# A long convolution and a state-space layer side by side: transposes moved to the DMA crossbar, wide VectorE operations, and the convolution's first stage spread out

## The chip, the cores and the metric

The kernel runs on one core of one Trainium2 chip. The metric is the device time of one execution in microseconds (us), median of several runs.

PE is the TensorE matmul engine (PEld its weight loads), DVE is VectorE, ACT ScalarE, POOL GpSimd and SP SyncE. SP and POOL mostly issue DMA here. SBUF and PSUM are the on-chip memories: the kernel keeps its operands in SBUF and its matmul results in PSUM. A crossbar transpose is a DMA instruction (`dma_start_transpose`) that transposes a matrix while it loads it. The granted clock is the share of its full clock that the profile shows for PE.

## The reference

Two independent layers over 2048 positions and 1024 channels, in bf16, written side by side into one output:

```python
# A: short shift convolution (4 taps), gate, 2048-long convolution by FFT, gate
k_shift = sum(k_pad[:, t:t + S] * shift_k[:, 3 - t] for t in range(4))
kv = k_shift * v
y  = irfft(rfft(kv, 2 * S) * rfft(ssm_k, 2 * S))[:S] + kv * ssm_D
a  = q * y
# B: complex diagonal state space, 1024 states
Bu = x @ B_bar.T                      # B_bar, Lam_bar from Lambda, B, dt
h[t] = Lam_bar * h[t - 1] + Bu[t]
b  = 2 * (h @ C.T).real + x * Dskip
out = concatenate([a, b], axis=-1)
```

## The kernel before

**Layer B** goes in 16 chunks of 128 positions. For each chunk: `pu = B x` on PE (128 matmuls of 128 columns), a rotation by the angles of the states on DVE, two real scans on DVE (`tensor_tensor_scan`, 2.28 us each), a rotation back, and `py = C h` on PE (512 columns wide). x, B and C must stand transposed in SBUF; PE does it:

```python
def b_xT(i, eng="s"):
    pt = ps_t.tile([P, ND, P], BF16, name="pt")
    for dd in range(ND):
        nc.tensor.transpose(pt[:, dd, :], xn[:, dd * P:(dd + 1) * P], ident[:])
    ...                                   # copied to xT by ACT
# bt_prep and ct_prep: the same for B (16 blocks) and C (16 blocks)
```

A rotation is six DVE operations (four multiplies, two adds), each 1024 wide, one half of it being

```python
nc.vector.tensor_mul(ta, u[:, 0], ci); nc.vector.tensor_mul(tb, u[:, 1], si)
nc.vector.tensor_add(ta, ta, tb)
...                                       # tb: the imaginary part, the same way
```

**Layer A** goes in three stages. A1: the taps (four multiplies, three adds and the gate, 1024 wide, on DVE), matmuls with DFT matrices, results `Ys_kv` and `Ys_h` stored to DRAM. A2: 32 groups; load `l2k`, `l2h`, matmul, product on DVE (two 1024-wide multiplies), matmul, store `Vs`. A3: 16 rows; load `vv` and `q`, matmul, multiply, store. Each stage reads back what the one ahead of it stored, so they run one after the other.

**The schedule** is a fixed list of ticks, 8 for each chunk of B. Instructions are emitted tick by tick and each engine runs its own in that order:

```python
A1_STEP, A1H_STEP, A2_STEP, A3_STEP = 2, 2, 2, 1      # ticks per row or group
# A1 rows at ticks 0, 2, 4 ...; A2 after A1; A3 after A2
for n2 in range(N2):                      # A1
    b = A1_T0 + int(n2 * A1_STEP)
    ...                                   # loads at b - 4, taps at b, matmuls at b + 2
A2_T0 = a1_last + 6
for g in range(NG):
    b = A2_T0 + g * A2_STEP
    ...
A3_T0 = a2_last + 8
```

So A1 takes ticks 0 to 33, A2 39 to 106, A3 114 to 131, and B ends at 136: the three stages of A are spread over the whole of B.

## Time and profile before

| | |
|---|---|
| time | 432.85 us (profiled execution: span 431.1) |
| first rotation starts / last gate multiply of A1 starts (DVE) | 37 / 171 us |
| first A2 matmul with `l2k` / last store of `Vs` issued | 193 / 363 us |
| last rotation starts a multiply with `ci` | 392 us |

Stretches of the kernel before: busy time of PE, PEld, DVE, ACT and POOL (with the number of instructions), granted TensorE clock, DMA share and GB/s, at the start and at the end:

```profile
0.00:20.00 20.00, 7.91 (x89) 7.04 (x90) 11.42 (x44) 10.27 (x12) 5.32 (x13) 0.99 0.84 264
20.00:40.00 20.00, 16.57 (x231) 15.28 (x231) 17.84 (x55) 15.59 (x32) 0.00 (x0) 0.83 0.82 270
40.00:60.00 20.00, 17.02 (x255) 14.95 (x253) 20.00 (x35) 18.62 (x28) 5.14 (x9) 1.00 0.96 329
60.00:80.00 20.00, 19.37 (x228) 15.09 (x226) 20.00 (x36) 20.00 (x33) 9.81 (x15) 1.00 0.84 274
...
400.00:420.00 20.00, 15.85 (x67) 6.38 (x66) 11.47 (x17) 9.48 (x18) 4.88 (x9) 0.91 0.94 361
420.00:440.00 20.00, 5.08 (x26) 2.18 (x24) 0.69 (x1) 1.31 (x3) 1.08 (x2) 0.91 0.10 39
```

PE's "busy" includes pipelined matmuls waiting on one another, so it hides slack. A sharper figure is the count of matmuls times the spacing at which they follow each other when nothing holds them up: 0.0558 us for 128 columns, 0.109 for 256, 0.2158 for 512, the means of the uninterrupted pairs in this trace. By that count the kernel has **357 us of matmul work in a span of 431**, so PE is idle for 74 us.

### The profile page before, as it was taken

How to read it: one execution, taken by the hardware profiler on the slowest of the kernel's cores; microseconds unless marked ns; L12 is line 12 of the kernel's file. 1: busy time of each engine (PE TensorE's matmuls, PEld its weight loads, DVE VectorE, ACT ScalarE, POOL GpSimd, SP SyncE). 2: the span in 40 equal slices, each digit the busy share in tenths (PEclk: the TensorE clock that was granted, in tenths of full speed). 3: DMA queues.
4: the chain of work that ended last, by engine and by line, in shares of the span. 5: the costliest groups of instructions: out<-in, count | busy, mean ns of one | idle time of the engine just before them, and what ended most of it. 6: DMA issues, size and time to landing. Idle time of an engine off the chain costs nothing.

```text
span 431.1 us, 9757 instructions
## 1 busy us (share of the span) xinstructions
PE 380.7 (88%) x3713; PEld 259.7 (60%) x3713; DVE 350.7 (81%) x642; ACT 303.6 (70%) x531; POOL 130.2 (30%) x224
## 2 busy tenths in 40 slices
PE   2589799797987997999899999999899999997784
PEld 2578687575765875775556566566465666763331
DVE  2989999999999999936897979797959637976830
ACT  1977999787886887646678877878568783344451
POOL 4000344464654455311222232322122211012121
PEclk9979999999999899999999999999899999999989
DMA  7879987778776544397778687879666523959981
GB/s 247 285 255 309 336 289 254 265 240 249 276 235 205 167 163 159 120 334 238 229 241 263 217 247 245 265 234 295 195 217 181 165 69 135 298 176 396 403 316 73
DMA packets 41353, 102.23 MB, mean 237 GB/s; under 512 B 6621, under 2 KB 8925, under 8 KB 41306
## 3 DMA queue, kind: packets, MB, share of 16 engines
q1 hardware_dynamic: 27322, 58.60, 42.7%
q0 software_dynamic: 13984, 43.01, 28.8%
q8 instruction: 29, 0.48, 0.5%
q14 instruction: 18, 0.15, 0.1%
HBM read 59.64 MB, written 33.55 MB: 216 GB/s over the span
## 4 chain that ended last, share of the span: by engine, by line
PE 42%; DVE 28%; issue 12%; DMA 10%; ACT 5%; POOL 2%; SPq 0%; POOLq 0%; DVEq 0%; ACTq 0%
PE pu L274 13%; PE py L345 13%; DVE m L409 5%; PE psa L508 5%; DVE acc L410 4%; DMA hb<-ha 3%; PE psa L533 3%; PE psa L532 3%; DVE ta L305 2%; DVE tb L308 2%; DVE acc L414 2%; DMA out_dram<-ot 2%; POOL out_dram L88 2%; DMA bn<-in_B_C_re_dram 1%; PE pt L601 1%
## 5 line engine op out<-in xcount | busy, mean ns | idle before, releaser
L274 PE MATMUL pu<-xT,BT 128*128 128x128 bf16 x2048 | 156.1, 222 | 0.5 <-ACT xT L263 0.3
L274 PEld LDWEIGHTS <-BT 128*128 128x128 bf16 x2048 | 136.2, 100 | 33.5 <-issue 2.4
L345 PE MATMUL py<-CT,h 128*128 128x512 bf16 x512 | 140.2, 382 | 2.3 <-ACT yo L355 2.3
L345 PEld LDWEIGHTS <-h 128*128 128x128 bf16 x512 | 46.7, 98 | 45.5 <-issue 4.9
L88 POOL DMA_DIRECT2D hb<-ha x64 | 33.4, 526 | 88.9 <-ACT ha L509 85.0
L534 ACT CAST vsb<-psa 128x512 bf16<-128x512 f32 x64 | 37.0, 602 | 25.7 <-PE psa L533 24.8
L88 POOL DMA_DIRECT2D Ys_h<-ysbh x64 | 45.6, 716 | 30.8 <-ACT ysbh L475 29.4
L277 ACT CAST u<-pu 128x512 bf16<-128x512 f32 x64 | 39.4, 615 | 13.2 <-PE pu L274 13.1
L428 ACT CAST ysb<-psa 128x512 bf16<-128x512 f32 x64 | 38.5, 644 | 13.7 <-PE psa L427 13.3
L519 DVE TENSOR_TENSOR ha<-x,ha 128x1024 bf16<-128x1024 bf16 x32 | 21.9, 684 | 27.8 <-DMA hb<-ha 18.7
L475 ACT CAST ysbh<-psa 128x512 bf16<-128x512 f32 x64 | 38.7, 641 | 5.5 <-issue 2.3
L509 ACT CAST ha<-psa 128x512 bf16<-128x512 f32 x64 | 36.8, 598 | 7.3 <-PE psa L508 6.3
L509 ACT CAST x<-psa 128x512 bf16<-128x512 f32 x64 | 36.9, 593 | 7.3 <-PE psa L508 5.2
L308 DVE TENSOR_TENSOR_SCAN tb<-rtab,tb 128x1024 bf16<-128x1024 f32 x16 | 36.6, 2285 | 0.0
L305 DVE TENSOR_TENSOR_SCAN ta<-rtab,ta 128x1024 bf16<-128x1024 f32 x16 | 36.5, 2280 | 0.0
L427 PE MATMUL psa<-acc,F1t 128*128 128x512 bf16 x64 | 24.6, 392 | 12.0 <-DVE acc L414 11.9
L564 ACT CAST ot<-psa 128x512 bf16<-128x512 f32 x32 | 17.9, 589 | 24.4 <-DMA out_dram<-ot 14.8
L409 DVE TENSOR_TENSOR m<-krow,wbc 128x1024 bf16<-128x1024 bf16 x48 | 32.4, 675 | 0.0
L410 DVE TENSOR_TENSOR acc<-acc,m 128x1024 bf16<-128x1024 bf16 x48 | 32.3, 673 | 0.0
L532 PE MATMUL psa<-ha,wts 128*128 128x512 bf16 x64 | 24.5, 384 | 4.2 <-DVE ha L519 4.0
L88 POOL DMA_DIRECT2D Ys_kv<-ysb x32 | 17.8, 557 | 33.9 <-ACT ysb L428 33.9
L350 PE MATMUL py<-Dd,xT 128*128 128x128 bf16 x128 | 28.0, 219 | 0.0
(139 smaller groups left out, 628.5 us busy)
## 6 DMA issues: line engine op xcount, KB each, us to landing
Ys_kv<-ysb POOLq DMA_DIRECT2D x32, 256.0 KB, 2.9
Ys_h<-ysbh POOLq DMA_DIRECT2D x64, 128.0 KB, 3.3
l2k<-Ys_kv SPq DMA_DIRECT2D x16, 512.0 KB, 6.0
l2h<-Ys_h SPq DMA_DIRECT2D x16, 512.0 KB, 4.2
hb<-ha POOLq DMA_DIRECT2D x64, 128.0 KB, 3.7
Vs<-vsb POOLq DMA_DIRECT2D x16, 512.0 KB, 5.9
vv<-Vs SPq DMA_DIRECT2D x32, 256.0 KB, 6.6
xn<-in_B_x_dram SPq DMA_DIRECT2D x16, 256.0 KB, 4.3
```

Source lines behind the costliest of these rows:

```text
L88: return nc.gpsimd.dma_start(out_, in_)
L274: nc.tensor.matmul(pu[:, c, jl, :], BT[:, j, c, dd, :], xT[:, dd, :], start=(dd == 0), stop=(dd == ND - 1))
L277: nc.scalar.copy(u[:, :, j - 1:j + 1, :], pu[:])
L305: ops.append(lambda: nc.vector.tensor_tensor_scan(fl(st["ta"]), fl(rtab), fl(st["ta"]), 0.0, ALU.mult, ALU.add))
L308: nc.vector.tensor_tensor_scan(fl(st["tb"]), fl(rtab), fl(st["tb"]), 0.0, ALU.mult, ALU.add)
L345: nc.tensor.matmul(py[:], h[:, c, j, :], CT[:, j, c, dh * 512:(dh + 1) * 512], start=(j == 0 and c == 0), stop=(j == NJ - 1 and c == 1))
L409: ops.append(lambda jj=jj: nc.vector.tensor_mul(st["m"][:], krows[n2 - jj][:], wbc[:, jj, :]))
L410: ops.append(lambda: nc.vector.tensor_add(st["acc"][:], st["acc"][:], st["m"][:]))
L428: nc.scalar.copy(ysb[:, dh * 512:(dh + 1) * 512], pt[:])
L475: nc.scalar.copy(ysbh[:, :, n2l, :], pt[:].rearrange("p (c d) -> p c d", c=2))
L509: nc.scalar.copy(d_[:, dh * 512:(dh + 1) * 512], pt[:])
L532: nc.tensor.matmul(pt[:], wts[:, gi, 1, :], ha[:, dh * 512:(dh + 1) * 512], start=True, stop=False)
```

## The change

The intent: take the transposes off PE and the copies behind them off ACT; make VectorE's operations fewer and wider; and, since A1 was limited by VectorE while PE waited, spread A1 over twice as many ticks so that both engines are used evenly.

```diff
-    def b_xT(i, eng="s"):            # PE transpose, copy by ACT
+    def b_load_x(i):
+        nc.sync.dma_start_transpose(xT[:], x[i * T:(i + 1) * T, :])
+    def bt_load(j, c):
+        nc.sync.dma_start_transpose(BT[:, j, c, :, :], Bv[c][:, j, :])
+    def ct_load(c, hf):
+        nc.sync.dma_start_transpose(CT[:, :, c, hf * 512:(hf + 1) * 512], Cv[c][hf * 512:(hf + 1) * 512, :])
+    U_PRO = cfg.get("u_pro", 3)      # was 1: chunks of pu in the prologue
...
+    def win(Z):                      # overlapping windows of one table: [Z0 Z1], [Z1 Z2]
+        z = Z[:].rearrange("p a j t -> p (a j t)")
+        return bass.AP(z.tensor, z.offset, [list(z.ap[0]), [W, 2], [1, 2 * W]])
+        def rot_mul(src, Z):         # one 4096-wide multiply in place of four
+            s_ = src[:].rearrange("p b j t -> p (b j t)").unsqueeze(1).to_broadcast([P, 2, 2 * W])
+            nc.vector.tensor_mul(m, s_, win(Z))
...                                   # then one 2048-wide add; the scans stay
+            nc.vector.tensor_mul(st["m"][:, 0:h0, :], kring[:, s0:s0 + h0, :], wbc[:, 0:h0, :])
...                                   # taps: k rows in a ring of 8, one multiply (two at the wrap)
+        nc.vector.tensor_mul(hab[:], x16[:].unsqueeze(1).to_broadcast([P, 2, D]), hab[:])
...
-    A1_STEP = cfg.get("a1_step", 2.0)
+    A1_STEP = cfg.get("a1_step", 4.0)
-    A1H_STEP = cfg.get("a1h_step", 2)
-    A2_STEP = cfg.get("a2_step", 2)
+    A1H_STEP = cfg.get("a1h_step", 4)
+    A2_STEP = cfg.get("a2_step", 1.75)
```

With these steps A1 takes ticks 0 to 63, A2 69 to 128, and A3 begins at tick 136, when B has ended. The number of `u` buffers falls from 5 to 4; PSUM moves one buffer from the transposes to A (3 to 4).

## The prediction

> **What bounds the kernel now.** The stretch table shows five stages. 0–37 us, prologue: weights loaded and transposed on PE. 37–180, stage A1: DVE is busy 141.6 of 143 us and is the limit; PE's matmuls wait for DVE's `acc`. 180–200: PE fills up with `pu`. 200–358, stage A2: PE busy 153 of 158 (DVE 126, ACT 121). 358–431, tail: B's last four chunks until about 405, and A3, which ends as a stream of loads and stores (DMA share 0.94 in 400–420).
>
> **What the change does.**
> - PE: 384 transposes go (xT, BT, CT). In the chain of waits 16 back-to-back 128-column matmuls take 0.89 us, so about 21 us of real PE time. Their copies leave ACT (42 us of records) and DVE (6 us). SP issues crossbar transposes instead, 12 MB in all.
> - DVE: a 1024-wide bf16 multiply takes 0.68 us of record, about 0.63 net of overlap. At 2 elements a cycle ("VectorE: DVE Perf Modes", side-by-side) I estimate 2.2 us for 4096 and 1.2 for 2048. The widened operands are rows re-read at step 0, which "Vector Engine (DVE) Microarchitecture Reference" section 5.1 says keep the double rate; this trace has no such bf16 case. A chunk's rotation falls from about 12.9 to 11.6 us (both 2.28 us scans stay), a tap step from 5.1 to 4.7, A2's product from 1.27 to 1.2: about 27 us less DVE in all, of 351.
> - Schedule: A1 lasts 8 chunks instead of 4.25 and overlaps more B. A3 now starts after B, alone.
>
> **Critical path (estimates).** Prologue, three chunks of `pu`: first rotation at 38 us. A1: 8 × (11.6 + 2 × 4.7) = 168 us, DVE-bound; PE has about 150 us there. Switch: 9. A2: 88 us PE-bound while `pu` runs (2.5 us a tick), then 52 us at DVE's 2.15 us a tick; it ends near 353. Tail: last store of Vs 6 us, first load 6, 16 MB at about 380 GB/s 42: 52 us. Total 405. The gain is mostly balance: PE idles less behind DVE in A1, and 21 us of PE and 27 us of DVE work are gone; about 20 us is given back because A3 no longer overlaps B.
>
> **Prediction: 405 us, 80% range 384 to 430. Faster by over 2%: 0.80; within 2%: 0.13; slower by over 2%: 0.07.**
>
> **What would show each step right or wrong.**
> - 4096-wide multiplies at 2.2–2.3 us, not 4.3.
> - DVE busy near 320 us, at least 95% of A1, which lasts 165–175 us.
> - About 3330 PE matmuls; A2 with PE above 90% at first, then DVE.
> - In the tail PE nearly idle, DMA above 0.85, 45–60 us from the last `vsb` store to the end.
> - Crossbar transposes of 256 KB landing 1 to 1.5 us apart. "DMA: Bandwidth & Descriptors" gives 261 GB/s effective; this trace shows none.
>
> **What would make it wrong.** The transposes are the largest risk: at 100 GB/s the prologue's 4.75 MB and CT's 4 MB behind it on the same queue would hold back the first `pu`, the parameters (their transpose now stands behind the first `pu` matmuls) and the fourth chunk's x (behind CT), on which PE's fixed order waits before A1's matmuls: 440 or more. If wide operands lose the double rate, the kernel is far slower. If A2, where PE, ACT and DVE are within about 10% of each other, couples badly through four PSUM buffers, add 10–15 us. A shorter tail or quicker prologue gives 385.

## More of the kernel before

The kernel before takes 432.85 us in the runs taken with the kernel after. In the later sessions, on five chips, it took 430.3 to 434.4 us. Each experiment is therefore compared with the kernel before **of its own session**.

The page of the kernel before: the engines (busy time, share of the span, instructions), then the span in 40 slices of 10.8 us (each digit is the busy share in tenths):

```profile
PE 380.7 (88%) x3713; PEld 259.7 (60%) x3713; DVE 350.7 (81%) x642; ACT 303.6 (70%) x531; POOL 130.2 (30%) x224
...
PE   2589799797987997999899999999899999997784
...
DVE  2989999999999999936897979797959637976830
ACT  1977999787886887646678877878568783344451
...
DMA  7879987778776544397778687879666523959981
```

DVE is full from slice 2 to 17 (the prologue's end and A1), and PE from then on. PE's row stays at 7 to 9 up to slice 39. That is because B's last chunks lie on top of A3.

Two groups of instructions of the kernel before, by line (busy us, mean ns of one):

```profile
L519 DVE TENSOR_TENSOR ha<-x,ha 128x1024 bf16<-128x1024 bf16 x32 | 21.9, 684 | 27.8 <-DMA hb<-ha 18.7
...
L409 DVE TENSOR_TENSOR m<-krow,wbc 128x1024 bf16<-128x1024 bf16 x48 | 32.4, 675 | 0.0
```

## The result, and the profile after

The kernel after takes **452.38 us** against 432.85: 4.8% **slower**. The result is correct. Ratios, here and below, are the mean time of one kernel's fast runs over that of the other's of the same rounds, so not quite the ratio of the medians; here it is 1.0479 (95% interval 1.043 to 1.053).

The page of the kernel after, the same rows as before (40 slices of 11.2 us):

```profile
PE 374.3 (83%) x3329; PEld 242.8 (54%) x3329; DVE 329.8 (73%) x339; ACT 269.0 (60%) x496; POOL 133.5 (30%) x231
...
PE   0567919899899899979999699899999879985773
...
DVE  0374399999999999999999494997878888302221
ACT  1098306567477575838564478868889677823342
...
DMA  7999999967554856444367959868889894569993
```

The removed work is gone: 384 matmul records fewer, ACT 35 us and DVE 21 us less. But PE's row begins later and has a hole at slice 6, and DVE's row is low until slice 5 and again in the last six.

Groups of the kernel after, by line, answering to the two of before:

```profile
L524 DVE TENSOR_TENSOR hab<-x,hab 128x2048 bf16<-128x2048 bf16 x32 | 39.0, 1222 | 32.1 <-DMA hab<-hab 25.1
...
L303 DVE TENSOR_TENSOR mt<-u,Z 128x4096 bf16<-128x4096 bf16 x16 | 36.6, 2286 | 5.1 <-ACT u L288 5.0
...
L407 DVE TENSOR_TENSOR mt<-kring,wbc 128x4096 bf16<-128x4096 bf16 (+3 forms) x16 | 30.3, 1892 | 0.9 <-DMA kring<-in_A_k_dram 0.3
```

The wide operations run as predicted: 2.29 us for 4096 elements and 1.22 for 2048, against 0.68 for 1024.

Stretches of the kernel after, start and end:

```profile
0.00:20.00 20.00, 3.36 (x29) 2.96 (x30) 1.17 (x10) 1.49 (x2) 9.00 (x20) 1.00 0.91 176
20.00:40.00 20.00, 16.29 (x209) 15.62 (x207) 12.39 (x56) 15.52 (x25) 0.00 (x0) 0.83 1.10 191
40.00:60.00 20.00, 13.23 (x178) 12.68 (x176) 11.00 (x18) 9.35 (x20) 0.49 (x1) 0.83 1.18 229
60.00:80.00 20.00, 14.10 (x179) 13.24 (x179) 19.47 (x16) 8.15 (x15) 4.03 (x6) 0.74 1.06 253
...
400.00:420.00 20.00, 12.79 (x35) 3.37 (x33) 4.15 (x6) 7.41 (x14) 3.80 (x7) 0.66 1.01 378
420.00:440.00 20.00, 14.11 (x32) 3.23 (x32) 5.54 (x8) 8.21 (x16) 4.08 (x8) 0.57 1.05 400
```

In the first 80 us the DMA engines show a busy share of 0.91 to 1.18 (the profile's figure can pass 1) and move 176 to 253 GB/s, less than before (264 to 329). After 400 us they move 378 to 400 GB/s with 32 to 35 matmuls in 20 us: that is A3 nearly alone (B's last matmul with C starts at 401 us), at a DMA share of 1.01 to 1.05.

The waits of PE in the first 80 us of the kernel after (us in total, times, longest). The 13.7 us are the wait for the very first x; the first `pu` matmul of the kernel before started at 12.2 us, so little of that one is new:

```profile
PE pu L285 <- DMA xT<-in_B_x_dram: 21.8, 2, 13.7
PE pu L285 <- DMA BT<-in_B_B_im_dram: 4.6, 2, 2.9
```

**Where the 18.5 us of span went.** By the count of matmul spacings, the kernel after has 336 us of matmul work in 449.6, so 114 us idle against 74:

| | before | after | difference |
|---|---|---|---|
| matmul work | 357 | 336 | −21 |
| PE idle, first 80 us | 29 | 46 | +17 |
| PE idle, 80 to 400 us | 32 | 33 | +2 |
| PE idle, after 400 us | 13 | 35 | +21 |
| span | 431 | 450 | +19 |

(The differences are of the unrounded values.) Idle here is all time beyond the count at full spacing, so a slower PE counts as idle too. The granted clock was lower after the change: 0.74 to 0.83 from 20 to 80 us (before: 0.83, then 1.00), and 0.66 and 0.57 after 400 us (before: 0.91). An estimate from the start times of the matmul records in the two traces: matmuls that followed one another at up to 2.25 times their spacing took 11 us beyond it in the first 80 us against 5 before, and 7 against 2 after 400 us. So some 5 us of each loss may be a slow clock. Whether the clock follows the waits or adds to the loss, no run tests.

The change saved what it promised on PE. By this count it lost it at the start, and as much again at the end. A count of idle time does not show which of it moves the end; the experiments ask that.

### The profile page after: what moved, and what is told of

The parts are those of the page before. It is cut to its first block, busy times and chain, and to the rows that moved or that the text cites. A ratio compares the mean times of both kernels' runs of the same rounds, so it can differ in the third digit from the quotient of the medians.

```text
span 449.6 us, 8585 instructions
## 1 busy us (share of the span) xinstructions
PE 374.3 (83%) x3329; PEld 242.8 (54%) x3329; DVE 329.8 (73%) x339; ACT 269.0 (60%) x496; POOL 133.5 (30%) x231
## 5 line engine op out<-in xcount | busy, mean ns | idle before, releaser
L285 PE MATMUL pu<-xT,BT 128*128 128x128 bf16 x2048 | 146.5, 229 | 28.4 <-DMA xT<-in_B_x_dram 21.8
L321 DVE TENSOR_TENSOR_SCAN g<-rtab,g 128x1024 bf16<-128x1024 f32 x32 | 72.6, 2282 | 0.3
L524 DVE TENSOR_TENSOR hab<-x,hab 128x2048 bf16<-128x2048 bf16 x32 | 39.0, 1222 | 32.1 <-DMA hab<-hab 25.1
L88 POOL DMA_DIRECT2D hab<-hab x64 | 33.3, 525 | 88.8 <-ACT hab L517 74.5
L537 ACT CAST vsb<-psa 128x512 bf16<-128x512 f32 x64 | 36.5, 611 | 21.8 <-PE psa L536 18.2
L483 ACT CAST ysbh<-psa 128x512 bf16<-128x512 f32 x64 | 37.2, 626 | 14.8 <-PE psa L482 11.3
L571 DVE TENSOR_TENSOR ot<-ot,qt 128x1024 bf16<-128x1024 bf16 x16 | 11.1, 692 | 41.4 <-ACT ot L567 41.4
L517 ACT CAST hab<-psa 128x512 bf16<-128x512 f32 x64 | 36.5, 606 | 6.9 <-PE psa L516 5.8
L303 DVE TENSOR_TENSOR mt<-u,Z 128x4096 bf16<-128x4096 bf16 x16 | 36.6, 2286 | 5.1 <-ACT u L288 5.0
L303 DVE TENSOR_TENSOR mt<-g,Z 128x4096 bf16<-128x4096 bf16 x16 | 36.5, 2281 | 0.0
L535 PE MATMUL psa<-hab,wts 128*128 128x512 bf16 x64 | 25.1, 393 | 11.5 <-DVE hab L524 11.4
L407 DVE TENSOR_TENSOR mt<-kring,wbc 128x4096 bf16<-128x4096 bf16 (+3 forms) x16 | 30.3, 1892 | 0.9 <-DMA kring<-in_A_k_dram 0.3
```

The source lines that it names most:

```text
L88: return nc.gpsimd.dma_start(out_, in_)
L285: nc.tensor.matmul(pu[:, c, jl, :], BT[:, j, c, dd, :], xT[:, dd, :], start=(dd == 0), stop=(dd == ND - 1))
L303: nc.vector.tensor_mul(m, s_, win(Z))
L321: nc.vector.tensor_tensor_scan(g[:, a * W:(a + 1) * W], rt1, g[:, a * W:(a + 1) * W], 0.0, ALU.mult, ALU.add)
L407: nc.vector.tensor_mul(st["m"][:, 0:h0, :], kring[:, s0:s0 + h0, :], wbc[:, 0:h0, :])
L483: nc.scalar.copy(ysbh[:, :, n2l, :], pt[:].rearrange("p (c d) -> p c d", c=2))
```

## The experiments

Two theories stood at first. **S**: the schedule is the loss; spreading A1 pushes A2 and A3 back until A3 runs alone. **X**: the crossbar transposes are the loss; they deliver late and slow down the loads beside them. Fifteen kernels were run. Chips differ by up to 1%, so the ratio to the same session's kernel before is given with each time.

### 1. The change with the old steps

```diff
-A1_STEP 4.0, A1H_STEP 4, A2_STEP 1.75
+A1_STEP 2.0, A1H_STEP 2, A2_STEP 2
```

> The changed kernel with only the schedule of stage A1 and A2 put back (a tap step and an h step every 2 ticks, a product step every 2 ticks), so that A3 again overlaps the last chunks of B. Theory S (the spread leaves A3 alone at the end with PE idle): A1 shrinks from 171 us to about 125, A2 starts near 200 and ends near 350, the end comes about 60 us after A2's end; 410 to 420 us, 7 to 9% faster than the changed kernel (452). Theory X (the crossbar transposes are what costs): within 2% of the changed kernel, about 450. First rotation stays near 53 us under both.

Measured: **454.9 us, ratio 1.0524** (1.045 to 1.060), correct. Theory S's 410 to 420 us failed outright. Undoing the schedule alone gives nothing. A1 now takes 141 us (52.9 to 193.6) against 134 in the kernel before (37 to 171), though its VectorE operations cost less. The waits of this kernel between 60 and 140 us show the stall:

```profile
DVE hT L469 <- ACT hT L465: 11.5, 2, 7.3
...
PE pu L285 <- DMA xT<-in_B_x_dram: 7.6, 1, 7.6
...
DVE mt L407 <- DMA kring<-in_A_k_dram: 3.6, 1, 3.6
```

PE stood still for a late x (58 to 66 us). DVE's waits for `hT` come at 95 to 102 us and before 137 us; that the late x sets them off through PE's fixed order is not shown by this trace. Experiment 6, the same steps with ordinary loads, shows that they belong to the crossbar: there the wait for the fourth x falls to under 1 us, the wait for `hT` falls from 11.5 to 3.4 us, and A1 takes 12 us less.

### 2. The change with ordinary loads instead of crossbar transposes (wrong result)

```diff
-nc.sync.dma_start_transpose(xT[:], x[i * T:(i + 1) * T, :])
+nc.sync.dma_start(xT[:], x[i * T:(i + 1) * T, :].rearrange("p (a b) -> p a b", a=ND))
 # B and C the same way; same bytes, same tiles, not transposed
```

> Wrong result on purpose: the changed kernel with every crossbar transpose (x, B, C) replaced by an ordinary load of the same bytes into the same tile; all else is unchanged. Theory X: the first rotation moves from 52.7 us to about 38 to 40, DMA share in the first 80 us falls well below 1, PE no longer waits for x, and the whole kernel gains 12 to 20 us (432 to 440). Theory S: at most 5 us gained, because the end is set elsewhere. If the gain is 12 to 20 us and not more, the transposes explain only a part.

Measured: **441.03 us, ratio 1.0218** (1.015 to 1.029). The result is wrong as intended. The first rotation starts at 45.8 us instead of 52.7, and in the first 40 us the loads move 269 and 366 GB/s instead of 176 and 191. The 7 us at the first rotation reach the end of A1 (216 us instead of 224), and A2 ends 10 us earlier (384 instead of 394). So the crossbar costs 11 us against transposes that cost nothing at all; both time and first rotation lie a little outside the ranges of theory X (432 to 440, and 38 to 40). That is a bound and no alternative: a correct kernel has to transpose somehow. And 9 us of loss remain.

### 3. The kernel before with the new steps alone

```diff
-A1_STEP 2.0, A1H_STEP 2, A2_STEP 2
+A1_STEP 4.0, A1H_STEP 4, A2_STEP 1.75      # b = A2_T0 + int(g * A2_STEP)
```

> The kernel before with only A1 spread over 64 ticks and A2 at 1.75 ticks (nothing else of the change). Theory S: A1 lasts 8 x (12.9 + 2 x 5.1) = 185 us, ends near 222, A2 starts near 244 and ends near 395, A3 alone 55 us: 445 to 460 us, 3 to 6% slower than before. Theory X: the schedule alone is neutral or better, 425 to 435.

Measured: **447.45 us, ratio 1.0344** (1.028 to 1.041), correct. The schedule alone costs the kernel before 15 us. Theory S is right in this direction.

### 4. The kernel before with the wide VectorE operations alone

The rotations, taps and A2's product of the change, with PE transposes and the old steps. To make room, `u` has 4 buffers, the ring of k rows 6, and the rows of x, B and C share one pool.

> The kernel before with only the wide DVE operations (rotations over the Hankel tables, 4096-wide taps, 2048-wide product); transposes stay on PE, A1 stays at 34 ticks. To fit in memory it has 4 buffers for u, freed early, a tap ring of 6 rows, and x, B and C rows share 4 buffers. Theories S and X both expect the DVE-bound A1 stage to shrink by about 12 us (141 to 129) and the tail's rotations by about 5: 413 to 422 us, 3 to 4% faster. The rival that the wide operations are themselves what costs (they hold the engine for 2.3 us and delay the short ones that others wait for): 430 or more.

Measured: **427.35 us, ratio 0.9896** (0.984 to 0.996), correct. A1's last gate multiply starts at 163 us instead of 171, 8 us earlier, but the first A2 matmul with `l2k` only 1.5 us earlier (191.2 against 192.7), and the whole gains 5 (4.5 by the ratio). That lies between the two expectations, 413 to 422 and 430 or more. In between PE's record is full (39.6 of 40 us busy in 160 to 200; 37.2 before), which suggests that PE limits there and that most of VectorE's gain only lets VectorE wait.

### 5. The change with a faster A2

```diff
-A2_STEP 1.75
+A2_STEP 1.25
```

> The changed kernel with one number altered: a product step of A2 every 1.25 ticks instead of 1.75, so that A2 ends about 2 chunks of B earlier and A3 has B's last chunks beside it again. Theory S (the tail where only A3 is left costs about 20 us of idle PE): A2 takes about 125 us instead of 148, ends near 370, the tail is 60 to 68 us: 430 to 440 us. Rival (A2 is held by its own chain of product, swap DMA and copies, so it cannot run faster, whatever the step says): A2's end stays near 390 and the time near 450.

Measured: **436.58 us, ratio 1.0143** (1.008 to 1.021), correct: about 15 us gained by one number (3.4 points of ratio). Last stores of `Vs`, after the change and here (line, count, duration, first and last start):

```profile
L88 POOL DMA_DIRECT2D Vs<-vsb x16: 538/572/574, 265.2 to 394.2; - x16
```

```profile
L88 POOL DMA_DIRECT2D Vs<-vsb x16: 537/572/574, 266.9 to 381.9; - x16
```

A2 ends 12 us earlier, and A3 now lies over B's last chunks: its loads start at 385 us and B's last matmul with C at 421 us (after the change: 397 and 401). The time from the last store of `Vs` to the end is the same, 56 us against 55. So B's last chunks fit beside A3 at no cost. The cost of leaving A3 alone at the end is thereby shown, not only argued.

### 6. Ordinary loads and the old steps together (wrong result)

The edits of 1 and 2 in one kernel.

> Wrong result on purpose: ordinary loads in place of the crossbar transposes together with the A1 and A2 steps of the kernel before. The crossbar version of this schedule took 455 us, 17 us above what I expected of A1 (141 against 125) and 22 above in A2. If the slow crossbar loads in the first 70 us are the reason that the dense A1 fails: A1 back to 125 to 130 us, 415 to 425 in all. If the smaller buffers (one PSUM buffer for transposes, four for u) or DVE's fixed order are the reason: A1 still 135 us or more, 440 or more.

Measured: **433.59 us, ratio 1.0071** (1.001 to 1.013). A1 takes 129 us (46.1 to 174.8), as the first expectation said, but the time missed its 415 to 425. Under the old steps the crossbar costs about 20 us (4.5 points of ratio), not 11: the parts of the change do not add. And transposes that cost nothing still leave this kernel 1.75 points, some 7 us, behind the one of experiment 4, which transposes on PE. That remainder is not the crossbar's; the two differ in the prologue (three chunks against one), its order, the PSUM buffers and the ring of k rows, and no run separates these.

### 7. The change with a one-chunk prologue

```diff
-U_PRO = cfg.get("u_pro", 3)
+U_PRO = cfg.get("u_pro", 1)
```

> The changed kernel with one chunk of u in the prologue instead of three; the crossbar loads are the same. If the first rotation waits for the landing of the last B tile (about 40 us): it stays at 43 to 46 us, 7 to 9 earlier than 52.7, and A1 ends that much earlier; the rest is unchanged, so 443 to 448. If the two chunks that are no longer prepared leave PE behind in A1 (DVE waits for u): no gain or a loss, 450 to 460.

Measured: **465.48 us, ratio 1.0809** (1.077 to 1.085), correct. The first rotation starts at 42.5 us, ten earlier, and the kernel is still about 14 us slower. PE has 33 matmul records in 40 to 60 us against 178: the three-chunk prologue is what PE has to do while transposes land. A1 ends 5 us later (228 us against 224), since DVE waits inside it, for u (4.9 us) and for k rows (6.4 us). So an earlier first rotation is worth something where the next chunks' u is ready, as in experiment 2, and nothing where it is not, as here.

### 8. Crossbar for C and for x after the first chunk, PE for the rest

Built on 4 (wide operations, old steps).

> The wide DVE operations with the schedule of the kernel before; B and the first x tile still transposed on PE, C and the other x tiles by crossbar. It takes 248 of the 384 transposes (about 14 us of PE) and about 34 us of ACT copies out of a kernel that PE limits after its first 200 us, and keeps the prologue's path free of crossbar loads. If the change's parts are sound and only their prologue and schedule are not: 410 to 418 us (before_wide 427). If crossbar loads cost as much as they save wherever they stand (a DMA queue held for 4 to 8 us by each C tile, late x): 425 or more.

Measured: **431.75 us, ratio 1.0012** (0.997 to 1.006), correct: about 5 us slower than 4 (1.16 points of ratio), though 14 us of PE and some 30 us of ACT work were taken away. Stretches of this kernel (the profiled run was its slowest, 436.5 us):

```profile
40.00:60.00 20.00, 13.88 (x182) 11.84 (x180) 19.83 (x17) 9.99 (x19) 5.08 (x8) 0.91 1.18 236
60.00:80.00 20.00, 14.92 (x121) 10.19 (x121) 11.04 (x12) 10.40 (x20) 7.33 (x11) 0.83 1.07 303
```

The DMA engines are full while C is transposed, and DVE has work for only 11 of 20 us in the second stretch (it waited 6.8 us for k rows). In this arrangement the crossbar gains nothing net. That it loses at the loads beside it what it saves on the engines is read from these stretches and not tested.

### 9. The transposes by themselves (a measuring kernel, wrong result)

```python
for i in range(16): nc.sync.dma_start_transpose(xt[i][:], xv[i])       # 256 KB each
for i in range(15, -1, -1): nc.sync.dma_start(xt[i]..., xv[i])         # the same bytes, plain
for i in range(15, -1, -1): nc.sync.dma_start_transpose(xt[i][:], xv[i])
# sixteen ordinary loads of k, 256 KB each, on the POOL queue
```

> A measuring kernel, wrong result on purpose, no comparison of times wanted: sixteen 256 KB crossbar transposes of x with nothing beside them, then the same 4 MB by ordinary loads on the same queue, then the transposes again with ordinary loads of k on the other queue. Theory X (the crossbar itself has a low rate, whatever runs beside it): the first phase takes 26 to 32 us, 130 to 160 GB/s, as the first 37 us of the changed kernel did, the ordinary loads 12 to 16 us, and the third phase is hardly longer than the first. Rival (the crossbar is as fast as ordinary loads by itself, and lost its rate in the changed kernel to the loads beside it): the first phase takes under 18 us, and only the third falls to 140 GB/s.

The loads of k were meant to stand beside the third phase, but 14 of the 16 were issued in the first 18 us, so the phases changed places: the **first** has loads beside it, the **third** nearly none. Landings are read from the small VectorE copy that waits for each tile (start, duration):

```profile
0.74 39.58 SPq L95 DMA_TRANSPOSE xt<-in_B_x_dram  x16
...
5.00 0.15 DVE L91 CAST z<-xt 128x1 f32<-128x1 bf16 x1 [5.00 <-DMA xt<-in_B_x_dram]
...
25.99 0.15 DVE L91 CAST z<-xt 128x1 f32<-128x1 bf16 x1 [3.52 <-DMA xt<-in_B_x_dram]
...
49.79 0.15 DVE L91 CAST z<-xt 128x1 f32<-128x1 bf16 x1 [0.50 <-DMA xt<-in_B_x_dram]
50.46 0.15 DVE L91 CAST z<-xt 128x1 f32<-128x1 bf16 x1 [0.51 <-DMA xt<-in_B_x_dram]
...
63.03 0.15 DVE L91 CAST z<-xt 128x1 f32<-128x1 bf16 x1 [0.80 <-DMA xt<-in_B_x_dram]
...
78.12 0.15 DVE L91 CAST z<-xt 128x1 f32<-128x1 bf16 x1 [0.91 <-DMA xt<-in_B_x_dram]
```

- Beside loads: the first 4 transposes took 26 us, while 3.7 MB of k went through. Together that is 4.7 MB at about 182 GB/s: the loads, too, went far below their own rate.
- After the loads, in the same phase: the other twelve landed from 25.99 to 42.72, 1.39 us apart. So the slow stretch went with the loads and not with the place of the phase.
- Nearly alone: from 63.03 to 78.12 eleven more landed, 1.37 us each, **191 GB/s**.
- Ordinary loads: from 49.79 to 55.87 nine landed, 0.68 us each, **388 GB/s**.

Both theories of the rate were half right. In this one run the crossbar by itself has half the rate of ordinary loads, and beside ordinary loads it falls far behind. The kernel after fits both (issues on SP's queue: start, duration):

```profile
2.20 1.34 SPq L139 DMA_TRANSPOSE BT<-in_B_B_re_dram  x1
3.58 3.31 SPq L133 DMA_TRANSPOSE xT<-in_B_x_dram  x1
6.93 4.35 SPq L139 DMA_TRANSPOSE BT<-in_B_B_im_dram  x1
11.31 5.47 SPq L133 DMA_TRANSPOSE xT<-in_B_x_dram  x2
16.84 1.31 SPq L139 DMA_TRANSPOSE BT<-in_B_B_re_dram  x1
18.19 1.31 SPq L139 DMA_TRANSPOSE BT<-in_B_B_im_dram  x1
...
38.83 8.03 SPq L142 DMA_TRANSPOSE CT<-in_B_C_re_dram  x1
```

Up to 16.8 us SP got five transposes out, beside the first loads on the other queue. From then on it issued one every 1.35 us (one took an us longer), the pace of the measuring kernel. The 19 transposes of x and B, 5.0 MB, thus took 35 us.

### 10. The change with the fourth and fifth x ahead of C

```diff
-                at(tu - 12, "misc", lambda i=i: b_load_x(i))
+                if i >= U_PRO + 2:
+                    at(tu - 12, "misc", lambda i=i: b_load_x(i))
...
+    for i in (U_PRO, U_PRO + 1):
+        b_load_x(i)
     for hf in range(2):
         for c in range(2):
             ct_load(c, hf)
```

> The changed kernel with the x of the fourth and fifth chunk transposed ahead of the four 1 MB transposes of C instead of behind them. The tensor engine waited 8.0 us for the fourth chunk's x at 58 to 66 us. If that wait is on the way to the end, 446 to 450 us instead of 452; if the time before the first rotation and the loss of overlap at the end are all that counts, it stays within 2 us of 452.

Measured: **452.2 us, ratio 1.0478** (1.042 to 1.054), correct: nothing. PE's wait for that x is gone (its 21.8 us for x in the first 80 us fall to 16.4, all of it the first x), and by the count PE does 5 us more work there; A1 still ends at 223 us. So these 5 us of idle PE were not on the way to the end.

### 11 and 12. A better pace: A2 at 1.5 ticks, A3 at 2

```diff
-A2_STEP 2, A3_STEP 1
+A2_STEP 1.5, A3_STEP 2
```

On the kernel with wide operations (4):

> The kernel before with the wide VectorE operations (427.4 us), A2 at 1.5 ticks a group instead of 2 and A3 at 2 ticks a row instead of 1, so that A3 begins some 16 ticks earlier and its loads are spread over the end of B. If the idle time of the tensor engine at the end (A3 alone or in a rush) is worth what it was worth in the changed kernel with a faster A2 (16 us), 415 to 422 us; if that gain was only the mending of the spread A1, 425 to 430 us.

On the kernel before, as the control:

> The control for it: the kernel before with the same two steps (A2 1.5, A3 2), nothing else. If pacing alone brings the gain, 420 to 427 us and the wide operations add 5 us again; if VectorE limits this stage in the kernel before (its narrower operations need more time per tick), no gain, 430 to 436 us.

Measured: with wide operations **421.43 us, ratio 0.9778** (0.971 to 0.985); the kernel before with two numbers changed **421.96 us, ratio 0.9783** (0.973 to 0.984). Both are correct and beat both kernels of this study. Both intervals lie below 1, but reach beyond 0.98. A3 now starts 16 ticks earlier and its loads are spread over B's last chunks. PE's row of the kernel with wide operations, which stays at 9 to the last slice but two:

```profile
PE   2577897989889789999799999999999999999984
```

The wide operations add nothing here: 0.5 us is within the spread. The expectation that they would add 5 us again was wrong.

### 13. Wide operations, PE transposes, the new steps

What was open after twelve runs: the loss had been divided between schedule and transposes only by a sum over kernels that each missed two parts, and one kernel gave wrong results. This run is kernel 4 with the new steps:

```diff
-A1_STEP 2.0, A1H_STEP 2, A2_STEP 2
+A1_STEP 4.0, A1H_STEP 4, A2_STEP 1.75
```

> The changed kernel's schedule (A1 and its kernel side over 64 ticks, A2 at 1.75) and its wide VectorE operations, but x, B and C transposed on the tensor engine with a one-chunk prologue as before. If the parts add (432, 15 for the spread, less 5 for the wide operations): 440 to 444 us, and the transposes with their prologue cost 8 to 12 us of the changed kernel. If the schedule loses the whole of it, 449 to 453 us.

Measured: **451.86 us, ratio 1.0434** (1.037 to 1.050), correct. The sum of parts (440 to 444) was wrong; the second alternative holds. With wide operations the new schedule costs 5.4 points of ratio, about 23 us, and what the crossbar and its prologue add on top of it (1.0479) is within the spread. The two traces show why that sum is near nothing. The change starts its first rotation 15 us later (52.7 against 37.9), but its A1 is 7 us shorter (171 against 178) and its A2 8 us (149 against 157); the switch between them (22 us) and the tail (55 us) are alike. So what the change brought besides (less work on PE and ACT, chunks prepared ahead, other buffers) was worth about 15 us, and the late start took them. Which of these bought them was not tested. Last stores of `Vs` in this kernel and in experiment 3:

```profile
L88 POOL DMA_DIRECT2D Vs<-vsb x16: 537/572/574, 255.0 to 394.5; - x16
```

```profile
L88 POOL DMA_DIRECT2D Vs<-vsb x16: 540/574/574, 253.9 to 391.6; - x16
```

With these steps A2 ends at 392 to 395 us, and A3 alone takes 55 us more, in all three correct kernels, whatever transposes and whatever the width of the VectorE operations.

### 14 and 15. The change at other paces

A1 over 48 ticks (steps 3), A2 1.5, A3 2:

> The changed kernel with A1 over 48 ticks (steps 3), A2 at 1.5 and A3 at 2 ticks a row. If the transposes cost some 11 us whatever the schedule, it ends at 431 to 437 us, against 421 to 422 us of the kernel before with its best pace; if a balanced schedule hides them, at 420 to 426 us.

Measured: **437.48 us, ratio 1.0091** (1.003 to 1.016), correct. That is the first expectation, just above its range: the pace does not hide the transposes.

The very pace of experiments 11 and 12 (A1 2, A2 1.5, A3 2):

> The changed kernel with A1 and its kernel side at 2 ticks as before, A2 at 1.5 and A3 at 2 ticks a row: the same pace as the two kernels that reached ratios of 0.978. If the crossbar transposes and the three-chunk prologue cost next to nothing net, 421 to 426 us, ratio 0.975 to 0.985; if they cost what the first rotation came late (15 us) and the stall on the fourth chunk's x adds to it, 437 to 445 us, ratio 1.01 to 1.03.

Measured: **441.71 us, ratio 1.021** (1.015 to 1.027), correct. At the pace at which PE transposes reach 0.978, the crossbar and its prologue cost 4.3 points, about 19 us. The waits of this kernel between 80 and 120 us show the same wait of DVE as in experiment 1, again at 95 to 102 us:

```profile
DVE hT L469 <- ACT hT L465: 7.7, 1, 7.7
ACT ysbh L483 <- DMA Ys_h<-ysbh: 6.7, 3, 3.5
```

### Together

All with wide VectorE operations and correct results; ratio to the kernel before of the session:

| pace (A1, A2, A3) | PE transposes, one-chunk prologue | crossbar, three-chunk prologue |
|---|---|---|
| 2, 2, 1 (that of before) | 0.9896 | 1.0524 |
| 2, 1.5, 2 | **0.9778** | 1.0210 |
| 4, 1.75, 1 (that of the change) | 1.0434 | **1.0479** (the change) |

Read down the left column, the new pace costs 5 points. Read across the two upper rows, the crossbar with its prologue costs 4 to 6 (the columns also differ in PSUM buffers and in the ring of k rows); of the 6.3 of the first row, 4.5 are the crossbar's and 1.75 are not (experiment 6). In the last row the two ways to transpose come out the same. Neither is free there: with ordinary loads in their place (experiment 2, wrong result) the ratio is 1.0218.

## Why the prediction was wrong

The lines of the two traces for the first rotation and for A2's first matmul with `l2k`, before and after (durations in ns, then first and last start):

```profile
L292 DVE TENSOR_TENSOR ta<-u,ci x16: 672/684/693, 37.3 to 392.5; 128x1024 bf16<-128x1024 bf16 x16
L508 PE MATMUL psa<-l2k,wts x64: 376/379/631, 192.7 to 353.3; 128*128 128x512 bf16 x64
```

```profile
L303 DVE TENSOR_TENSOR mt<-u,Z x16: 2283/2284/2292, 52.7 to 361.5; 128x4096 bf16<-128x4096 bf16 x16
L516 PE MATMUL psa<-l2k,wts x64: 376/379/631, 245.4 to 388.4; 128*128 128x512 bf16 x64
```

The predicted sum and what the trace has for its terms:

| term | predicted | measured |
|---|---|---|
| first rotation | 38 | 52.7 |
| A1, to the last tap | 168 | 170.8 (52.7 to 223.5) |
| switch to A2's first matmul with `l2k` | 9 | 21.9 (to 245.4) |
| A2, to the last store of `Vs` | 138 | 148.8 (to 394.2) |
| tail, A3 alone | 52 | 55.4 (to 449.6) |
| sum | 405 | 449.6 |

The sum was 45 us short: 15 in the prologue, 13 in the switch, 11 in A2, 3 in A1 and 3 in the tail. So the failed steps are the first rotation at 38 us, the switch of 9 us and A2; A1 and the tail held.

- **Right: the wide operations, and A1.** "VectorE: DVE Perf Modes" (section "Side-by-side: where the cycles go for N=2048 bf16") and "Vector Engine (DVE) Microarchitecture Reference" (section 5.1, a row read again and again) of the Trainium skill let the double rate be expected. The trace agrees, 2.29 us for 4096 elements, also with the overlapping windows of one table as the other operand. A1 is VectorE-bound at 39.5 of every 40 us, as predicted. VectorE's total fell by 21 us, not 27.
- **Right as a mechanism: the tail.** It is A3 nearly alone, at 378 to 400 GB/s and a DMA share of 1.01 to 1.05. PE was not "nearly idle" by its record (12.8 and 14.1 of 20 us), but that was at a granted clock of 0.66 and 0.57.
- **Wrong: "First rotation at 38 us."** The prediction named the transposes as its largest risk, but carried in its sum a prologue no later than before. Of the Trainium skill, "DMA: Bandwidth & Descriptors" (section "Latency and other measured facts") gives 261 GB/s for transposes with a non-contiguous middle dimension, and "Advanced Engine Details and Errata" (section "X-Bar Transpose (TRN2)") says that they are "as fast as regular DMAs". Measured were 191 GB/s nearly alone, and about 142 in the prologue, partly beside other loads (5.0 MB in 35 us). The measurement decides. The prediction's own test, landings 1 to 1.5 us apart, was met in the measuring kernel (1.37 us), and in the kernel after the issues kept 1.35 us from 16.8 us on; nineteen at that pace would be 26 us. The other 9 were lost at the start, where five transposes took 15 us beside the first loads. But the crossbar explains only half of the 15 us: with ordinary loads the first rotation still starts at 45.8 (experiment 2), 8 us late. With one chunk in the prologue it starts at 42.5 (experiment 7), so the three chunks have a share in it; how the 8 us divide stays open. Of the harms that the prediction listed under this risk, the late x of the fourth chunk came true (8.0 us), but it did not move the end (experiment 10).
- **Wrong: the switch, 9 us.** It is 22 us after, and it was so before: from 171 to 193 us. After the last tap come its matmuls (to 229.8 us), the store of `Ys`, a load of `l2k` issued only at 237.3, and about 6 us until it lands (the median is 6.1). The trace of the kernel before showed this chain and could have been used.
- **A2 mis-sized by 11 us.** It was put at PE's and VectorE's rates, with no loss for waits such as those on `hab`: PE's second matmuls waited 11.5 us, nearly all of it for that. How much of the 11 us these waits make was not tested.
- **The step that failed in the argument: "The gain is mostly balance: PE idles less behind DVE in A1 … about 20 us is given back because A3 no longer overlaps B."** The give-back was seen and its size was near: 21 us more idle PE after 400 us, some 5 of which may be the lower clock. The gain to be set against it was not there. From 80 to 400 us PE idles as long as before (33 and 32 us). Experiment 4 suggests why so little was to be had: with A1's end 8 us earlier, A2 began 1.5 us earlier, while PE's record was full in between. Experiments 3 and 13 show the schedule as a plain loss, of 15 us with narrow and 23 with wide operations, when it stands without the crossbar.
- **The saved work was real, and the late start took it back.** At the same pace and with PE transposes (experiment 13) the first rotation starts 15 us earlier, and A1 and A2 together take 15 us longer: the end is the same. Experiment 2 shows crossbar transposes, against loads of the same bytes, as the cause of 11 us; experiment 7 shows that without the longer prologue it would have been worse.

What stays open: why the schedule costs 23 us with wide operations and 15 with narrow ones (the two also differ in the number of `u` buffers); what the lower granted clock adds; and how the 19 us of experiment 15 divide between the crossbar's own rate and the loads that it slows down.

## What to carry to other kernels

When stages must run one after the other and another layer runs beside them, ask for the engine that limits the sum (here PE) when it has nothing to do. A stage that stands alone at the end is paid in full, and moving two pacing numbers so that it overlaps was worth more (10 us, correct, in the unchanged kernel) than taking 21 us of work off PE. Not all idle time counts, though: experiment 10 filled some and won nothing. Work taken off a busy engine and given to DMA is not free: check first at what rate the DMA does it beside the loads already there. And two losses need not add: test each part with the others as they were, and also with the others as they will be.

## What the Trainium skill lacked or had wrong

- "Advanced Engine Details and Errata", section "X-Bar Transpose (TRN2)": crossbar transposes as fast as regular DMAs, 350 to 400 GB/s expected. With 256 KB each on one queue the runs show 191 GB/s nearly alone against 388 for ordinary loads of the same bytes on the same queue.
- "DMA: Bandwidth & Descriptors", section "Latency and other measured facts": 261 GB/s with a non-contiguous middle dimension, 350 to 400 when contiguous. Neither was reached here. The page says nothing of the rate of transposes beside ordinary loads: 4 of 256 KB in 26 us while 3.7 MB of loads went through.
- No page has the time for which a transpose of such a size holds the issuing queue on this chip (one page has a count of cycles, for small tiles): in the first 75 us of the kernel after, SP issues one of 256 KB in 1.31 us undisturbed and in up to 4.35 us otherwise, one of 1 MB in 4.1 to 8.0 us, and an ordinary load of 256 KB in 0.33 to 0.65 us.
- "Vector Engine (DVE) Microarchitecture Reference", section 5.1, lists input rows that overlap as not measured. Here a bf16 multiply of 4096 elements with two overlapping rows of 2048 as one operand, and a row read twice as the other, took 2.29 us, the double rate (1024 elements: 0.68 us).
